# The expert gate's small tiles move into PSUM, its table behind the scatter, its diagonals to ScalarE

## The chip, the cores and the metric

The kernel runs on one core of a Trainium2 chip. The metric is the device time of one launch in microseconds (us), lower is better. The kernel before takes 684.4 us, the median of three runs (684.36 to 685.31).

## What is computed

Three stages follow each other. A clustered attention: 2 batches of 8 heads, 768 tokens, head dimension 64; a query attends only to keys whose nearest centroid (16 per head) is its own. A mixture of 8 experts with one expert per token. A second, dense layer with mish in the middle.

```python
scores = where(q_assign[..., :, None] == k_assign[..., None, :], q @ k.T / 8, -1e9)
x = softmax(scores) @ v                            # -> (1536, 512)
logits = x @ w_gate + modality_bias[modality_id]   # (1536, 8)
e_idx = argmax(logits); gate_w = softmax(logits)[e_idx]
out[e_idx == e] = gate_w * (relu(x @ w1[e]) @ w2[e])
h = out @ w_in                                     # (1536, 2048)
return (h * tanh(softplus(h))) @ w_out             # (1536, 512)
```

## The kernel before, in words

Almost every product is made of three f16 products (high part by high, low by high, high by low). In the attention, `st_step` makes 128 keys by 768 queries of scores on TensorE (L391), ScalarE takes the exponential (L393) and its f16 part (L400), GpSimd subtracts for the low part `el` (`psub`, L114), and TensorE multiplies with v (L425 to L429). After a head, `fin` divides on VectorE (L440 to L442, tile `xt`), ScalarE makes the f16 part (L445) and GpSimd the low part (L447). The centroid work of a head (`assign`) runs three heads ahead: maxima on VectorE (L286 to L292), two GpSimd operations (L295, L296), a VectorE transpose (L299), a ScalarE copy (L301) and four small DMAs into `QK` (L303).

After each pair of heads `pregate` adds a quarter of the logits of a batch: transposes, matmuls into a PSUM tile `lg`, two VectorE operations into the SBUF tile `l`. When the last quarter of a batch is in, `gate(b)` runs once for that batch of 768 tokens (128 partitions by 6 tiles). It takes the row maximum and the exponential, a one-hot `oh` of the best expert, counts with matmuls of `ones` and a triangle `tri` into the PSUM tile `rk` (L748 to L751), the gate weight `g` (L754 to L760, written into the extra columns of the token rows), and the experts' order by size (`key`, `kp`, `gt`, `st`); from these comes `pu`, the sorted row of every token (L782). Six indirect DMAs of GpSimd scatter the rows of `xb` to the DRAM tensor `dr` (L802). Besides, it makes the expert numbers `ei` (L789), by which ScalarE's or SyncE's queue loads expert weights (`w_load`, L900, L912), and the table `tab`, `nblk` and `mask` (L798 and L810 to L822), which is needed when the sorted rows are back and at the very end. The rows come back by SyncE's queue in order (L832, tile `xs`), and `sorted_mm` turns them with matmuls against two diagonal matrices `dg` of the gate weight (`diag`, L702; matmuls L713) into `xw`, the input of the experts.

`gate(0)` runs while the attention of batch 1 goes on; `gate(1)` runs after the attention, beside the experts of batch 0 (`moe1`: matmuls L1007, ScalarE L965 and L918, VectorE L969 and L922), the first matmuls of the dense layer (`h_units`, `mish` L1106 to L1115) and the conversion of `w_out` (L1027 to L1035). In the code the order of these strands is fixed by generators; within it a planner orders the instructions of each engine by its own estimate of when they are ready, except SyncE's, which stay as written. Every engine then executes its queue in that order, and an instruction that waits holds up all that is behind it.

`eps` is a PSUM pool of two banks that the attention's side work, the gate of batch 0 and the experts share; for batch 1 the gate uses a bank of the pool `ps_2`.

Of the kernel before, what the change touches and what calls it, by code (L numbers as in the profile page):

```python
# [8 lines left out]
F16 = mybir.dt.float16  # L9
F32 = mybir.dt.float32  # L10
# [3 lines left out]
AF = mybir.ActivationFunctionType  # L14
ALU = mybir.AluOpType
# [4 lines left out]
P = 128  # L20
# [4 lines left out]
def clustered_attention_moe_kernel(  # L25
# [84 lines left out]
    def eps(shape, dt=F32):  # L110
        return ps_e.tile(shape, dt, tag="e", name="eps")
# [11 lines left out]
    ident16 = cp.tile([P, P], F16, name="ident16")  # L123
# [324 lines left out]
        fin_done.add(i)  # L448
        yield

    lg_t = {}
    pre_done = set()

    def pregate(b, c):

        x = xb[b]
        last = (b, c) == (B - 1, CD - 1)

        def bank(shape, dt=F32):
            if last:  # L460
                return ps_x.tile(shape, dt, tag="x", name="x")
            return eps(shape, dt)

        xT = lp.tile([P, 2, S], F16, tag="xT", name="xT")
        for a in range(2):
            pt = bank([P, 1024], F16)
            for t in range(T):
                nc.tensor.transpose(pt[:, t * P:(t + 1) * P], x[:, t, a * DM + c * P:a * DM + (c + 1) * P], ident16)
            yield 2
            if a < XTA:  # L470
                nc.scalar.activation(out=xT[:, a], in_=pt[:, 0:S], func=AF.Copy)
            else:
                nc.vector.tensor_copy(xT[:, a], pt[:, 0:S])
            yield 1 + 3 * a
        lg = bank([P, T, 2 * E])
        for t in range(T):
            nc.tensor.matmul(lg[:, t, :], lhsT=xT[:, 0, t * P:(t + 1) * P], rhs=wg[:, c, :], start=(t == 0), stop=False, skip_group_check=True)
            nc.tensor.matmul(lg[:, t, 0:E], lhsT=xT[:, 1, t * P:(t + 1) * P], rhs=wg[:, c, 0:E], start=False, stop=(t == T - 1), skip_group_check=True)
        yield 2
        isc = 2.0 ** -14  # L480
        if c == 0:
            lg_t[b] = g1.tile([P, T, E], F32, tag="l", name="l", bufs=2)
        l = lg_t[b]
# [214 lines left out]
    def diag(xs):  # L698
        sc = xs[:, 2 * DM:].bitcast(F32)
        dg = g1.tile([P, 2, P], F16, tag="dg", name="dg", bufs=2)  # L700
        for a in range(2):
            nc.vector.tensor_scalar(out=dg[:, a], in0=ident16, scalar1=sc[:, 1 + a:2 + a], scalar2=None, op0=ALU.mult)  # L702
        return dg

    def sorted_mm(xs, dg, xr, c0, parts, pool=None):
# [16 lines left out]
    def gate(b):  # L722
# [2 lines left out]
        l = lg_t[b]  # L725
        G = lambda nm, shape, dt=F32: g1.tile(shape, dt, tag=nm, name=nm)
        V = nc.vector
        mx = G("gmx", [P, T, 1])
        V.reduce_max(out=mx[:, :, 0], in_=l, axis=AX.X)
        d = G("gd", [P, T, E])  # L730
        mb_ = mx.to_broadcast([P, T, E])
        V.tensor_tensor(out=d, in0=l, in1=mb_, op=ALU.subtract)
        nc.scalar.activation(out=d, in_=d, func=AF.Exp)
        eq = G("geq", [P, T, E])
        V.tensor_tensor(out=eq, in0=l, in1=mb_, op=ALU.is_equal)
        V.tensor_tensor(out=eq, in0=eq, in1=desc8[:, None, :].to_broadcast([P, T, E]), op=ALU.mult)
        m2 = G("gm2", [P, T, 1])
# [1 line left out]
        oh = G("goh", [P, T, E], F16)  # L739
        V.tensor_tensor(out=oh, in0=eq, in1=m2.to_broadcast([P, T, E]), op=ALU.is_equal)  # L740
        yield
        if b:
            rk = m_p["ps"].tile([P, 512], F32, tag="o", name="o", bufs=NQ)
        else:
            rk = eps([P, 512])
        r3 = rk[:, 0:T * E].rearrange("p (t e) -> p t e", e=E)
        for t in range(T):
            nc.tensor.matmul(rk[:, 64:64 + E], lhsT=ones, rhs=oh[:, t, :], start=(t == 0), stop=False, skip_group_check=True)  # L748
# [12 lines left out]
        V.memset(xf[:, :, 3], 0.0)  # L761
        yield

        cnt = rk[:, 64:64 + E]
# [7 lines left out]
        V.tensor_tensor(out=gt, in0=kp[:, None, :].to_broadcast([P, E, E]), in1=kp[:, :, None].to_broadcast([P, E, E]), op=ALU.is_gt)  # L772
# [12 lines left out]
        V.tensor_copy(c_, cnt)  # L785
# [9 lines left out]
        V.tensor_scalar(out=bst, in0=ma[:, 1:2], scalar1=-1.0, scalar2=float(S), op0=ALU.mult, op1=ALU.add)  # L795
        sel = [G(f"ge{k_}", [P, E]) for k_ in range(2)]
        for k_ in range(2):
            V.tensor_scalar(out=sel[k_], in0=key, scalar1=m8[:, k_:k_ + 1], scalar2=None, op0=ALU.is_equal)  # L798
        ab = G("gab", [P, E])
        prev = []  # L800
        for t in range(T):
# [5 lines left out]
                yield  # L807
        be = slice(b * E, (b + 1) * E)
        tl, te = tab[:, 0, be], tab[:, 1, be]
        V.scalar_tensor_tensor(out=tl, in0=sel[0], scalar=float(W), in1=st[:, 0, :], op0=ALU.mult, op1=ALU.add)  # L810
        V.tensor_tensor(out=te, in0=st[:, 0, :], in1=c_, op=ALU.add)
        V.tensor_scalar(out=ab, in0=sel[1], scalar1=-float(W), scalar2=float(S), op0=ALU.mult, op1=ALU.add)
        V.tensor_tensor(out=te, in0=te, in1=ab, op=ALU.min)
        V.tensor_tensor(out=ab, in0=te, in1=tl, op=ALU.subtract)
        V.tensor_scalar(out=ab, in0=ab, scalar1=0.0, scalar2=float(P - 1), op0=ALU.max, op1=ALU.add)
        V.tensor_copy(nblk[:, be], ab)
        V.tensor_scalar(out=nblk[:, be], in0=nblk[:, be], scalar1=7, scalar2=None, op0=ALU.logical_shift_right)
        if b:
            V.tensor_scalar(out=tab[:, :, be], in0=tab[:, :, be], scalar1=float(b * S), scalar2=None, op0=ALU.add)
        mask = G("gmask", [P, 2, OV], F16)  # L820
        V.tensor_scalar(out=mask[:, 0, :], in0=mcol, scalar1=ma[:, 0:1], scalar2=None, op0=ALU.is_lt)
        V.tensor_scalar(out=mask[:, 1, :], in0=mcol, scalar1=bst, scalar2=None, op0=ALU.is_ge)  # L822
        yield "sorted"
        ids = lp.tile([P, T], U32, tag="ids", name="ids", bufs=2)
        ids_t[b] = ids
# [187 lines left out]
    m_p = {}  # L1013
# [358 lines left out]
```

## Time and profile before

| | |
|---|---|
| median of 3 runs | 684.4 us |
| the profiled execution | 684.2 us, of which the span from first to last instruction is 682.4 us |
| TensorE (PE) busy | 622.8 us, 91% |
| VectorE (DVE) busy | 384.9 us, 56% |
| ScalarE (ACT) busy | 447.6 us, 66% |
| GpSimd (POOL) busy | 255.9 us, 37% |
| mean granted TensorE clock | 0.974 |

The times below are us from the start of the span. Busy shares are means over stages with different limits, so the stages of the two gates (about 159 to 196 us, and 324 to 363 us) are read by themselves.

### The profile page before, as it was taken

How to read it: one execution, taken by the hardware profiler on the slowest of the kernel's cores; microseconds unless marked ns; L12 is line 12 of the kernel's file. 1: busy time of each engine (PE TensorE's matmuls, PEld its weight loads, DVE VectorE, ACT ScalarE, POOL GpSimd, SP SyncE). 2: the span in 40 equal slices, each digit the busy share in tenths (PEclk: the TensorE clock that was granted, in tenths of full speed). 3: DMA queues.
4: the chain of work that ended last, by engine and by line, in shares of the span. 5: the costliest groups of instructions: out<-in, count | busy, mean ns of one | idle time of the engine just before them, and what ended most of it. 6: DMA issues, size and time to landing. Idle time of an engine off the chain costs nothing. (4 is left out here: it accounts for less than half of the span.)

```text
span 682.4 us, 13665 instructions
## 1 busy us (share of the span) xinstructions
PE 622.8 (91%) x5474; PEld 424.2 (62%) x5475; DVE 384.9 (56%) x767; ACT 447.6 (66%) x680; POOL 255.9 (37%) x226
## 2 busy tenths in 40 slices
PE   1698989989798998998989889999999999999995
PEld 1376768857476676565866556566666667676442
DVE  5768666788789799889567899622311101101000
ACT  4687798876776666665777778665655576767300
POOL 5466776875864243330421222111311232222211
PEclk9889999989789899899999999999999999999998
DMA  7632363312862243555346554212000000000000
GB/s 221 157 74 65 89 168 94 90 41 64 283 190 74 87 143 110 169 149 161 117 129 225 177 155 157 93 33 62 32 1 1 4 29 0 32 1 16 17 32 34
DMA packets 56741, 64.41 MB, mean 94 GB/s; under 512 B 10080, under 2 KB 46944, under 8 KB 56672
## 3 DMA queue, kind: packets, MB, share of 16 engines
q1 hardware_dynamic: 42064, 48.74, 24.8%
q10 hardware_dynamic: 12688, 8.42, 4.1%
q0 software_dynamic: 1920, 6.32, 2.4%
q8 instruction: 45, 0.74, 0.4%
q14 instruction: 24, 0.20, 0.1%
HBM read 46.23 MB, written 6.32 MB: 77 GB/s over the span
## 5 line engine op out<-in xcount | busy, mean ns | idle before, releaser
L114 POOL TENSOR_TENSOR el<-e,eh 128x768 f16<-128x768 f32 x64 | 106.9, 1675 | 87.2 <-ACT eh L400 48.9
L1007 PE MATMUL h<-x,win 128*128 128x256 f16 x1152 | 132.0, 273 | 0.0
L1007 PEld LDWEIGHTS <-win 128*128 128x128 f16 x1152 | 112.5, 98 | 18.6 <-issue 0.2
L1007 PEld LDWEIGHTS <-w 128*128 128x128 f16 x768 | 75.2, 99 | 68.4 <-issue 13.8
L1112 DVE SCALAR_TENSOR_TENSOR s<-s,h 128x512 f32<-128x512 f32 x48 | 30.8, 684 | 148.1 <-ACT s L1108 145.5
L1163 PE MATMUL o<-wout,xb 128*128 128x512 f16 x432 | 95.9, 379 | 0.0
L114 POOL TENSOR_TENSOR xb<-s,xb 128x1024 f16<-128x1024 f32 x18 | 40.4, 2243 | 126.7 <-ACT xb L1115 126.6
L1007 PE MATMUL eps<-xw,w 128*128 128x416 f16 x384 | 75.2, 344 | 9.5 <-DVE hT L969 5.2
L391 PE MATMUL s<-QK 128*128 128x384 f16 x320 | 79.3, 339 | 3.5 <-ACT ef L393 1.6
L351 DVE TENSOR_REDUCE mxh<-x 128x1 f32<-128x512 f32 x96 | 64.7, 681 | 17.7 <-PE x L350 17.2
L1007 PE MATMUL eps<-hT,w 128*128 128x416 f16 x384 | 73.8, 344 | 0.8 <-DVE hT L969 0.8
L1163 PEld LDWEIGHTS <-xb 128*128 128x128 f16 x432 | 42.3, 98 | 48.3
L393 ACT ACTIVATE e<-s 128x384 f32<-128x384 f32 x112 | 52.4, 489 | 23.2 <-PE s L391 19.9
L400 ACT ACTIVATE eh<-e 128x768 f16<-128x768 f32 x64 | 54.0, 846 | 1.4 <-DVE w L922 0.7
L427 PE MATMUL av<-vst,eh 128*128 128x65 f16 x384 | 46.9, 196 | 5.3 <-DVE xt L442 4.9
L425 PE MATMUL av<-vst,ef 128*128 128x65 f32 x384 | 49.6, 272 | 0.0
L425 PEld LDWEIGHTS av<-vst,ef 128*128 128x128 f32 x384 | 48.0, 192 | 1.5
L429 PE MATMUL av<-vst,el 128*128 128x65 f16 x384 | 45.1, 195 | 2.9 <-POOL el L114 2.9
L428 PE MATMUL av<-vst,eh 128*128 128x64 f16 x384 | 47.1, 197 | 0.0
L922 DVE SCALAR_TENSOR_TENSOR w<-wf,w 128x1024 f16<-128x1024 f32 x32 | 43.9, 1373 | 5.6 <-ACT w L918 5.2
L1106 ACT ACTIVATE s<-h,cst 128x512 f32<-128x512 f32 x48 | 32.9, 686 | 21.4 <-PE h L1007 21.2
L391 PEld LDWEIGHTS <-QK 128*128 128x128 f16 x384 | 34.2, 103 | 19.9 <-issue 8.5
(223 smaller groups left out, 1095.7 us busy)
## 6 DMA issues: line engine op xcount, KB each, us to landing
wf<-in_moe_w_dram ACTq DMA_DIRECT2D x16, 512.0 KB, 3.6
raw<-in_moe_w_in_dram SPq DMA_DIRECT2D x16, 512.0 KB, 3.7
raw<-in_moe_w_out_dram SPq DMA_DIRECT2D x16, 512.0 KB, 4.2
wf<-in_moe_w_dram SPq DMA_DIRECT2D x16, 512.0 KB
QK<-hl SPq DMA_DIRECT2D x32, 192.0 KB, 5.7
xs<-dr SPq DMA_DIRECT2D x12, 258.0 KB, 3.9
t<-in_k_dram SPq DMA_DIRECT2D x8, 384.0 KB, 4.4
t<-in_q_dram SPq DMA_DIRECT2D x8, 384.0 KB, 3.6
```

Of the source, the lines that this page charges most:

```text
L114: nc.gpsimd.tensor_tensor(out=out_, in0=in0, in1=in1, op=ALU.subtract)
L351: nc.vector.reduce_max(out=mx_t[i][:, t, 0:1], in_=sp, axis=AX.X)
L391: nc.tensor.matmul(sps[hf][:, 0:HS], lhsT=st[:, KA + a, kt * P:(kt + 1) * P], rhs=st[:, QA + a, hf * HS:(hf + 1) * HS], start=(a == 0), st ...
L393: nc.scalar.activation(out=e32[:, hf * HS:(hf + 1) * HS], in_=sps[hf][:, 0:HS], func=AF.Exp, scale=1.0 / float(D) ** 0.5)
L400: nc.scalar.activation(out=eh, in_=e32, func=AF.Copy)
L425: nc.tensor.matmul(av[:, t, :], lhsT=e32[:, cols], rhs=vs[:, h, :], start=(kt == 0 and t == 0), stop=(kt == T - 1), skip_group_check=True)
L427: nc.tensor.matmul(av[:, t, :], lhsT=eh[:, cols], rhs=vs[:, h, 0:NV], start=(kt == 0 and t == 0), stop=False, skip_group_check=True)
L428: nc.tensor.matmul(av[:, t, 0:D], lhsT=eh[:, cols], rhs=vs[:, h, NV:], start=False, stop=False, skip_group_check=True)
L429: nc.tensor.matmul(av[:, t, :], lhsT=el[:, cols], rhs=vs[:, h, 0:NV], start=False, stop=(kt == T - 1), skip_group_check=True)
L922: nc.vector.scalar_tensor_tensor(out=hl_[:, 1], in0=f, scalar=32.0, in1=hl_[:, 0], op0=ALU.mult, op1=ALU.subtract)
L1007: nc.tensor.matmul(out_, lhsT=wc[:, a, kk, ms], rhs=mv[:, c, kk, :], start=(i == 0), stop=(i == n - 1))
L1163: nc.tensor.matmul(pts[t], lhsT=gsl[q % 2][f // FB][:, f % FB, a, t * P:(t + 1) * P], rhs=wout[:, c, f, :], start=(f == 0 and i_ == 0), st ...
```

## The change

The gate's tiles `mx`, `eq`, `g`, `key`, `kp`, `pe`, and the counts `rk` and `cnt`, become slices of one PSUM bank; for batch 0 that is the bank of the last quarter of the logits, which `pregate` now allocates whole, for batch 1 a bank of `ps_2`. Where an operation had `key` or `kp` as both inputs, a second copy is written to SBUF, and one input is read from there (two more VectorE instructions per gate). The instructions of the table are issued after the one that makes `pu`. The two diagonals per tile of 128 rows are made by ScalarE instead of VectorE.

```diff
 def pregate(b, c):
-        lg = bank([P, T, 2 * E])
+        lgb = bank([P, 512])
+        lg = lgb[:, 0:2 * T * E].rearrange("p (t e) -> p t e", e=2 * E)
...
+        if c == CD - 1 and not b:
+            lg_b[b] = lgb
 def diag(xs):
-            nc.vector.tensor_scalar(out=dg[:, a], in0=ident16, scalar1=sc[:, 1 + a:2 + a], scalar2=None, op0=ALU.mult)
+            nc.scalar.activation(out=dg[:, a], in_=ident16, func=AF.Copy, scale=sc[:, 1 + a:2 + a])
 def gate(b):
-        mx = G("gmx", [P, T, 1])
+        bk = lg_b.get(b)
+        if bk is None:
+            bk = m_p["ps"].tile([P, 512], F32, tag="o", name="o", bufs=NQ)
+        at = [2 * T * E]
+        def R(*shape):
...                       # the next free columns of bk
+        mx = R(T, 1)
-        eq = G("geq", [P, T, E])
+        eq = R(T, E)
...
-        if b:
-            rk = m_p["ps"].tile([P, 512], F32, tag="o", name="o", bufs=NQ)
-        else:
-            rk = eps([P, 512])
+        rk, cnt = R(T * E), R(E)
...
-        g = G("gg", [P, T])
+        g = R(T)
...
-        key = G("gkey", [P, E])
-        V.scalar_tensor_tensor(out=key, in0=cnt, scalar=float(E), in1=desc8, op0=ALU.mult, op1=ALU.add)
+        key, keys = R(E), G("gkey", [P, E])
+        for k_ in (key, keys):
+            V.scalar_tensor_tensor(out=k_, in0=cnt, scalar=float(E), in1=desc8, op0=ALU.mult, op1=ALU.add)
...
-        kp = G("gkp", [P, E])
-        V.scalar_tensor_tensor(out=kp, in0=key, scalar=m8[:, 1:2], in1=key, op0=ALU.not_equal, op1=ALU.mult)
+        kp, kps = R(E), G("gkp", [P, E])
+        for k_ in (kp, kps):
+            V.scalar_tensor_tensor(out=k_, in0=key, scalar=m8[:, 1:2], in1=keys, op0=ALU.not_equal, op1=ALU.mult)
-        V.tensor_tensor(out=gt, in0=kp[:, None, :]..., in1=kp[:, :, None]..., op=ALU.is_gt)
+        V.tensor_tensor(out=gt, in0=kp[:, None, :]..., in1=kps[:, :, None]..., op=ALU.is_gt)
...
-        pe = G("gpe", [P, T, E])
+        pe = R(T, E)
...
-        V.tensor_scalar(out=pu, in0=pf, scalar1=float(b * S), scalar2=None, op0=ALU.add)
+        pi = V.tensor_scalar(out=pu, in0=pf, scalar1=float(b * S), scalar2=None, op0=ALU.add)
...
-            V.tensor_scalar(out=sel[k_], in0=key, scalar1=m8[:, k_:k_ + 1], scalar2=None, op0=ALU.is_equal)
+            with tc.issue_after(pi.ins):
+                V.tensor_scalar(out=sel[k_], in0=key, scalar1=m8[:, k_:k_ + 1], scalar2=None, op0=ALU.is_equal)
...
+        with tc.issue_after(pi.ins):
             V.scalar_tensor_tensor(out=tl, in0=sel[0], ...)
...                       # and the rest of the table, to the two masks
```

## Rows read from the trace of the kernel before

**Rows 1.** The page's first part: busy us (share of the span), number of instructions.
```profile
PE 622.8 (91%) x5474; PEld 424.2 (62%) x5475; DVE 384.9 (56%) x767; ACT 447.6 (66%) x680; POOL 255.9 (37%) x226
```
**Rows 2.** Windows: stretch, length, busy us by engine, granted clock, DMA share, GB/s.
```profile
173.00:184.00 11.00, 7.17 (x37) 3.29 (x37) 8.30 (x13) 7.06 (x11) 9.46 (x8) 0.73 0.91 276
184.00:196.00 12.00, 11.72 (x132) 8.92 (x129) 7.80 (x20) 9.00 (x17) 11.60 (x9) 0.72 0.71 250
196.00:224.00 28.00, 24.30 (x325) 19.40 (x324) 26.98 (x62) 21.34 (x42) 12.08 (x10) 0.99 0.33 85
```
**Rows 3.** PE's timeline, first gate: start, us, operation [idle before <-releaser].
```profile
171.24 0.48 PE L391 MATMUL s<-QK 128*128 128x384 f16 x2 [1.01 <-ACT e L393]
...
174.90 0.58 PE L350 MATMUL x<-QK 128*128 128x512 f16 x1 [1.55 <-DMA QK<-oT]
...
183.78 0.20 PE L429 MATMUL av<-vst,el 128*128 128x65 f16 x1 [2.28 <-POOL el L114]
```
**Rows 4.** DVE's timeline in the first gate.
```profile
160.52 1.09 DVE L732 TENSOR_TENSOR gd<-l,gmx 128x48 f32<-128x48 f32 x1
...
163.38 1.58 DVE L758 TENSOR_SCALAR gh<-gg 128x6 f16<-128x6 f32 x1
...
166.38 1.06 DVE L798 TENSOR_SCALAR ge<-gkey,gm 128x8 f32<-128x8 f32 x2
...
168.75 1.08 DVE L791 TENSOR_SCALAR gi<-gi 128x2 int32<-128x2 int32 x1
...
171.81 0.17 DVE L782 TENSOR_SCALAR gpu<-gpf 128x6 uint32<-128x6 f32 x1
```
**Rows 5.** POOL's timeline in the first gate.
```profile
163.27 1.66 POOL L114 TENSOR_TENSOR el<-e,eh 128x768 f16<-128x768 f32 x1 [1.73 <-issue]
...
171.82 0.36 POOL L295 TENSOR_SCALAR so<-seq 128x192 f16<-128x192 f32 x1 [2.01 <-DVE gpf L780]
...
172.91 1.20 POOL L802 DMA_INDIRECT dr<-xb,gpu  x1 [0.29 <-DVE nblk L816]
...
182.06 4.86 POOL L114 TENSOR_TENSOR el<-e,eh 128x768 f16<-128x768 f32 x3
```
**Rows 6.** ACT's timeline in the first gate.
```profile
165.88 0.52 ACT L445 ACTIVATE xb<-xt 128x384 f16<-128x384 f32 x1 [1.99 <-DVE xt L442]
...
169.96 0.85 ACT L301 ACTIVATE oT<-oC 128x384 f16<-128x384 f16 x1 [1.92 <-DVE gi L791]
...
184.19 1.06 ACT L918 ACTIVATE w<-wf 128x1024 f16<-128x1024 f32 x1 [2.85 <-DMA wf<-in_moe_w_dram]
```
**Rows 7.** DVE's timeline in the second gate.
```profile
329.71 0.36 DVE L798 TENSOR_SCALAR ge<-gkey,gm 128x8 f32<-128x8 f32 x2
...
331.87 0.17 DVE L782 TENSOR_SCALAR gpu<-gpf 128x6 uint32<-128x6 f32 x1
...
332.56 0.17 DVE L817 TENSOR_SCALAR nblk<-nblk 128x8 int32<-128x8 int32 x1
```
**Rows 8.** POOL's timeline in the second gate.
```profile
332.80 1.08 POOL L802 DMA_INDIRECT dr<-xb,gpu  x1 [16.65 <-DVE nblk L817]
...
345.88 2.13 POOL L114 TENSOR_TENSOR xb<-s,xb 128x1024 f16<-128x1024 f32 x1 [3.42 <-ACT xb L1115]
```
**Rows 9.** PE's timeline when the sorted rows of batch 1 are back.
```profile
345.87 0.94 PE L713 MATMUL o<-dg,xs 128*128 128x128 f16 x12 [0.89 <-DVE dg L702]
348.11 0.94 PE L713 MATMUL o<-dg,xs 128*128 128x128 f16 x12 [1.31 <-DVE dg L702]
```
**Rows 10.** DVE's timeline at the same place.
```profile
346.37 1.85 DVE L702 TENSOR_SCALAR dg<-ident,xs 128x128 f16<-128x128 f16 x2 [0.33 <-DMA xs<-dr]
```
**Rows 11.** ACT's timeline at the same place.
```profile
346.15 1.06 ACT L918 ACTIVATE w<-wf 128x1024 f16<-128x1024 f32 x1
```
**Rows 12.** Groups by line and shape: busy us, mean ns of one | idle before.
```profile
L702 DVE TENSOR_SCALAR dg<-ident,xs 128x128 f16<-128x128 f16 x24 | 6.5, 315 | 1.7 <-DMA xs<-dr 1.7
...
L717 ACT ACTIVATE xw<-o 128x128 f16<-128x128 f32 x1 | 0.3, 269 | 0.0
```

More of the change, by code (lines that the diff above doesn't have):

```diff
@@ L449, in fin @@
         yield
-    lg_t = {}
+    lg_t, lg_b = {}, {}
     pre_done = set()
@@ L727, in gate @@
         V = nc.vector
-        mx = G("gmx", [P, T, 1])
+        bk = lg_b.get(b)
[3 more added lines that the diff above has]
+        def R(*shape):
+            n_ = 1
+            for q_ in shape:
+                n_ *= q_
+            o_ = at[0]
+            at[0] += n_
+            assert at[0] <= 512
+            v_ = bk[:, o_:o_ + n_]
+            return v_ if len(shape) == 1 else v_.rearrange("p (a b) -> p a b", b=shape[1])
+        mx = R(T, 1)
         V.reduce_max(out=mx[:, :, 0], in_=l, axis=AX.X)
@@ L741, in gate @@
         yield
-        if b:
-            rk = m_p["ps"].tile([P, 512], F32, tag="o", name="o", bufs=NQ)
-        else:
-            rk = eps([P, 512])
-        r3 = rk[:, 0:T * E].rearrange("p (t e) -> p t e", e=E)
+        rk, cnt = R(T * E), R(E)
+        r3 = rk.rearrange("p (t e) -> p t e", e=E)
         for t in range(T):
-            nc.tensor.matmul(rk[:, 64:64 + E], lhsT=ones, rhs=oh[:, t, :], start=(t == 0), stop=False, skip_group_check=True)
+            nc.tensor.matmul(cnt, lhsT=ones, rhs=oh[:, t, :], start=(t == 0), stop=False, skip_group_check=True)
         nc.tensor.matmul(rk[:, 0:T * E], lhsT=tri, rhs=oh.rearrange("p t e -> p (t e)"), start=False, stop=False, skip_group_check=True)
@@ L762, in gate @@
         yield
-        cnt = rk[:, 64:64 + E]
-        key = G("gkey", [P, E])
-        V.scalar_tensor_tensor(out=key, in0=cnt, scalar=float(E), in1=desc8, op0=ALU.mult, op1=ALU.add)
+        key, keys = R(E), G("gkey", [P, E])
+        for k_ in (key, keys):
+            V.scalar_tensor_tensor(out=k_, in0=cnt, scalar=float(E), in1=desc8, op0=ALU.mult, op1=ALU.add)
         m8 = G("gm8", [P, 8])
         V.max(out=m8, in_=key)
-        kp = G("gkp", [P, E])
-        V.scalar_tensor_tensor(out=kp, in0=key, scalar=m8[:, 1:2], in1=key, op0=ALU.not_equal, op1=ALU.mult)
+        kp, kps = R(E), G("gkp", [P, E])
+        for k_ in (kp, kps):
+            V.scalar_tensor_tensor(out=k_, in0=key, scalar=m8[:, 1:2], in1=keys, op0=ALU.not_equal, op1=ALU.mult)
         gt = G("ggt", [P, E, E], F16)
-        V.tensor_tensor(out=gt, in0=kp[:, None, :].to_broadcast([P, E, E]), in1=kp[:, :, None].to_broadcast([P, E, E]), op=ALU.is_gt)
+        V.tensor_tensor(out=gt, in0=kp[:, None, :].to_broadcast([P, E, E]), in1=kps[:, :, None].to_broadcast([P, E, E]), op=ALU.is_gt)
         V.tensor_tensor(out=gt, in0=gt, in1=cnt[:, None, :].to_broadcast([P, E, E]), op=ALU.mult)
@@ L809, in gate @@
         tl, te = tab[:, 0, be], tab[:, 1, be]
[L810 to L822, printed above, removed]
+        with tc.issue_after(pi.ins):
+            V.scalar_tensor_tensor(out=tl, in0=sel[0], scalar=float(W), in1=st[:, 0, :], op0=ALU.mult, op1=ALU.add)
+            V.tensor_tensor(out=te, in0=st[:, 0, :], in1=c_, op=ALU.add)
+            V.tensor_scalar(out=ab, in0=sel[1], scalar1=-float(W), scalar2=float(S), op0=ALU.mult, op1=ALU.add)
+            V.tensor_tensor(out=te, in0=te, in1=ab, op=ALU.min)
+            V.tensor_tensor(out=ab, in0=te, in1=tl, op=ALU.subtract)
+            V.tensor_scalar(out=ab, in0=ab, scalar1=0.0, scalar2=float(P - 1), op0=ALU.max, op1=ALU.add)
+            V.tensor_copy(nblk[:, be], ab)
+            V.tensor_scalar(out=nblk[:, be], in0=nblk[:, be], scalar1=7, scalar2=None, op0=ALU.logical_shift_right)
+            if b:
+                V.tensor_scalar(out=tab[:, :, be], in0=tab[:, :, be], scalar1=float(b * S), scalar2=None, op0=ALU.add)
+            mask = G("gmask", [P, 2, OV], F16)
+            V.tensor_scalar(out=mask[:, 0, :], in0=mcol, scalar1=ma[:, 0:1], scalar2=None, op0=ALU.is_lt)
+            V.tensor_scalar(out=mask[:, 1, :], in0=mcol, scalar1=bst, scalar2=None, op0=ALU.is_ge)
         yield "sorted"
```

## The prediction, made before the changed kernel was run

> **What bounds the kernel now.** First the busy shares: TensorE is busy for 622.8 us, 91% of the span [rows 1], so any part that doesn't shorten TensorE's queue must be found in its pauses. Then the windows about the two gates: from 173 to 184 TensorE works for 7.17 of 11 us, and from there to 196 it is busy nearly throughout, but the granted clock is 0.73 and 0.72 in the two stretches [rows 2]. The clock has two levels, 1.2 and 2.4 GHz, so a mean of 0.72 says that over half of the stretch was granted the lower one, after pauses. Then TensorE's own timeline: inside the first gate it waits 1.01 us for an exponential of ScalarE, 1.55 us for a transfer of centroid rows and 2.28 us for GpSimd's low part [rows 3]. All three lie behind the gate only indirectly, through the queues of VectorE, ScalarE and GpSimd, so these were read next.
>
> VectorE shows what the change goes for. Operations on tiles of 48, 6, 16 and 2 elements per partition take 1.09, 1.58, 1.06 (two together) and 1.08 us [rows 4]; the same pair of L798 takes 0.36 in the second gate [rows 7]. Each long one ends when a GpSimd operation ends: L758 (163.38 + 1.58 = 164.96) with the low part that began at 163.27 and took 1.66 [rows 4, 5]. So a small VectorE operation whose tensors are all in SBUF waits for GpSimd's running one. I read that as a shared way into SBUF.
>
> ScalarE hands it on: L445 waits 1.99 us for `xt`, which VectorE makes behind L758; and L301 starts at 169.96 after 1.92 us of idle time that ends with L791 [rows 6]. GpSimd does so too: the scatter starts at 172.91, behind L295, which had waited 2.01 us for VectorE, and the next low parts come at 182.06, after six scatters [rows 5]; that is the 2.28 us at 183.78 [rows 3].
>
> In the second gate TensorE has work (the dense layer) until the sorted rows are back. There it waits 0.89 and 1.31 us for the diagonals [rows 9]. The second wait is the same stall: one of the two L702 that began at 346.37 ended at 348.22, after the GpSimd operation of 345.88 to 348.01 [rows 8, 10].
>
> **Part 1: small tiles in PSUM.** The stall goes where an operand is now in PSUM: `mx` (L732), `g` (L758), `key` (L798). With 0.18 us as the price of a free one (L798's pair gives 0.36) it removes 1.09 - 0.18 = 0.91, 1.58 - 0.18 = 1.40, and 1.06 - 0.36 = 0.70 us, 3.0 us of VectorE in the first gate [rows 4, 7]. L791's 0.9 stays, since `i2` remains in SBUF; so do the casts and scalings of `gh`, `ei`, `ma`, which happened to fall between GpSimd's operations and may not any more. The two added copies of `key` and `kp` cost at most 0.18 each, 0.36 per gate, and sit on the way to `pu`; at half of that, because such operations start before the one ahead has ended, 0.2. That an operation on a PSUM tile costs what it costs in SBUF is an assumption; both ends are a gain of nothing and a loss of 0.1 each over some 15 operations, 1.5 us, which I don't take, since L798's pair on SBUF has no better price to lose.
>
> In the second gate no GpSimd operation ran beside the gate's arithmetic (GpSimd had been idle for 16.65 us [rows 8]), so this part is worth nothing there and costs the 0.2.
>
> How much of the 3.0 reaches TensorE in the first gate? ScalarE's L445 can come earlier by what L732 and L758 lose, at most 2.3, but no more than its own wait of 1.99 [rows 6]. L301 stands behind it, and behind L791, which may stall as before: I bound its move by 0.3 and 1.9 and take 1.0, nearer the middle because half of the stalling operations stay. TensorE's waits of 1.01 and 1.55 hang on L393 and L301, so TensorE runs 1.0 earlier from there.
>
> **Part 2: the table behind `pu`.** Eight instructions leave the way to `pu` (two L798, six others). In the second gate that is 0.36 for the pair and at most 0.17 (L817) for each of the six [rows 7], 1.4 at the most; overlapped as above, 0.9. Less the 0.2 for the copies, `pu` is ready 0.7 earlier there. In the first gate it is 3.0 + 0.9 - 0.2 = 3.7 at the most, but the scatter is queued behind L295 and L296 [rows 5], whose input comes from VectorE's same queue; I take 2.0 between 1.0 (ScalarE's move alone) and 3.7. The six scatters then end 2.0 earlier, and so does the low part that TensorE waits for at 183.78.
>
> What is late next: TensorE, 1.0 earlier by part 1, would wait 1.3 instead of 2.28 and leave 2.0 earlier; but ScalarE stands at 184.19, where it has waited 2.85 for expert weights, and its 1.06 us hold back the exponentials behind it until 185.25 [rows 6]. That transfer is issued in ScalarE's queue behind the work of 174.90, so it moves by 1.0; and from 173 to 184 the DMA engines are busy for 0.91 of the time [rows 2], so it won't move by more. TensorE therefore keeps 1.0 and some of the rest: **1.3 us for the first gate** (bounds 0 and 3.0).
>
> In the second gate the scatter began at 332.80, 0.76 after `pu` (331.87 + 0.17) and 0.07 after L817 ended (332.56 + 0.17) [rows 7, 8]. Either the 0.76 is the way from a semaphore to GpSimd's first scatter, and it moves with `pu` by 0.7; or the scatter can't start while VectorE runs the table, and it doesn't move at all, since the table now lies wholly behind `pu`. I take 0.4.
>
> The Trainium skill speaks for the second: the page "SBUF — State Buffer", section "Who interferes with whom", says that VectorE and GpSimd share a pair of SBUF ports as a lock, that copies, casts and scalings which use both ports shut GpSimd out for the whole instruction, and that GpSimd can't write the descriptors of its own DMAs meanwhile. The 0.07 us at 332.73 agrees; the first rule, that one input in PSUM avoids the lock, is not shown by the kernel before for the gate's tiles. By that page the 0.4 would be zero, and the sum 0.4 smaller.
>
> **Part 3: diagonals by ScalarE.** Twenty-four instructions move. On VectorE the 24 take 6.5 us with one stall of 1.4 in them, so 0.22 each; a ScalarE copy of 128x128 from PSUM takes 0.269 [rows 12], 0.54 a pair. For batch 0 most pairs, I take four of six, fall in the stretch 196 to 224, where VectorE is busy for 26.98 of 28 us and ScalarE for 21.34 [rows 2]: ScalarE has 6.7 us to spare for 2.2, and VectorE gains 8 x 0.22 = 1.8. TensorE is busy 24.30 of 28 there, so at most that 1.8 comes out; ScalarE's exponentials are delayed by up to 0.54 at each pair, and four such are 2.2 lost. I take 0.2 gained.
>
> For batch 1 the stall of L702 goes, 1.85 - 0.44 = 1.4 [rows 10]. But ScalarE's queue has L918 from 346.15 to 347.21 [rows 11]; behind it the second pair is ready at 347.75, 0.36 to 0.5 before the 348.11 of [rows 9]; ahead of it, 1.3 before. The first pair loses 0.1. So 0.4 in all, and with the scatter's 0.4, **0.8 us for the second gate** (bounds: all of 0.7 + 1.3 = 2.0 gained; 0.9 lost if the first pair too is queued behind L918, as below).
>
> **Sum.** 1.3 + 0.2 + 0.8 = 2.3 us. The profiled execution took 684.2 (its span of 682.4 and 1.8 around it); 684.2 - 2.3 = 681.9. The median of the runs is 0.2 above the profiled one, so 682.1 us. It all comes through only because TensorE has no long wait for anything but its neighbours' queues later on, and these move with it.
>
> **Rivals.** *A slower kernel: ScalarE's queue takes the diagonals' wait.* A diagonal on ScalarE waits for the sorted rows, and the exponentials, expert weights and mish are behind it. If the first pair of batch 1 stands behind L918 it is ready at 347.21 + 0.54 = 347.75 instead of before 345.87: 1.9 lost, less the 1.3 of the second wait, which it absorbs, 0.6; for batch 0, 2.2 lost as above. With a first gate that yields its lower bound of 0.3 and `pu`'s 0.4 that makes 2.1 slower, 686.5, and some 685.9 if half of the pairs of batch 0 hurt. It decides where the planner puts a pair ahead of its rows' arrival, or behind a 1-us operation. For it: ScalarE is on the way to TensorE in the first gate twice [rows 3, 6]. Against: 6.7 us of spare time [rows 2].
>
> *No change that can be told.* The stalls move on to the tiles left in SBUF (L791 and its like), the weights' transfer at 184.19 holds the first gate where it is, and only 0.6 of the second gate is left: 683.8. For it: GpSimd is busy 9.46 of 11 us from 173 [rows 2] and so meets whatever VectorE issues; against: three of the four long ones are gone by construction.
>
> *The lock on the scatter,* as above, with less than the forecast in both gates (VectorE's table now beside six scatters instead of before them): 682.8.
>
> *The clock comes back.* If TensorE's pauses shrink enough that the clock stays up, the 12 us from 184 at 0.72 [rows 2] would take up to 12 x 0.28 = 3.4 less where TensorE is the limit; I take 2.6 more than the forecast: 679.5. Against: pauses of 1.0 and 1.55 us stay.
>
> **How the numbers follow.** Forecast 0.42, lock 0.10, clock 0.12, no change 0.19, slower 0.17. Faster means under 683.0 (0.2% of 684.4 is 1.4 us, about what a measurement tells from no change), slower over 685.8: nine tenths of the forecast, the clock and six tenths of the lock give 0.56 faster; 0.25 stays within; 0.19 is slower, with a little for orders of the planner that I can't see. The range that holds 8 in 10 leaves out half of the clock's case and most of the slower one: 678.8 to 685.6. The likeliest case's own range is 681.0 to 683.2.
>
> **What would show it.** Right: L732, L758 and L798 at 0.2 each beside a running GpSimd operation; L445's wait under 1; the first scatter of batch 0 near 171, of batch 1 near 332.3; TensorE's wait for the low part near 1.3; the wait of 1.31 for the second pair under 1. Wrong: VectorE operations of over 1 us on L759, L787 or L789; TensorE waiting for a diagonal from ScalarE for over 1 us; the first scatter again at the table's end. A result above 684.4 would mean that ScalarE, not VectorE, was what the gates leaned on.

## The result and the profile after

The changed kernel takes 680.25 us (median of 11 runs, 679.32 to 682.83). The kernel before, run beside it, took 687.09 (11 runs, 684.12 to 690.1; the three of the front page are among them). The ratio is **0.9911, 95% interval 0.9885 to 0.9937**: faster by 0.9%, 6.1 of 687.09 us, where 2.3 were forecast (a ratio of 0.9966). The profiled execution took 680.72.

The first part of the page, which answers to [rows 1]:

```profile
span 679.0 us, 13674 instructions
## 1 busy us (share of the span) xinstructions
PE 620.5 (91%) x5474; PEld 424.5 (63%) x5475; DVE 378.3 (56%) x747; ACT 454.6 (67%) x704; POOL 255.4 (38%) x226
```

VectorE is busy 6.6 us less, ScalarE 7.0 more: the diagonals. TensorE is busy 2.3 less with the same matmuls, which points at its clock. The stretches of [rows 2], in the same columns:

```profile
173.00:184.00 11.00, 7.47 (x58) 4.90 (x58) 8.08 (x22) 8.03 (x14) 8.35 (x7) 0.84 1.02 309
184.00:196.00 12.00, 10.44 (x144) 8.03 (x143) 10.35 (x22) 10.55 (x22) 10.63 (x9) 1.00 0.93 289
196.00:224.00 28.00, 24.20 (x315) 18.82 (x313) 23.34 (x50) 22.75 (x50) 13.54 (x10) 1.00 0.33 86
```

The clock of the first two is 0.84 and 1.00 where it was 0.73 and 0.72. Over the whole first gate, the kernel before and then the changed one:

```profile
150.00:196.00 46.00, 39.43 (x442) 28.10 (x440) 35.02 (x98) 31.54 (x57) 33.20 (x28) 0.83 0.56 175
150.00:196.00 46.00, 39.38 (x501) 30.34 (x502) 35.27 (x103) 34.06 (x64) 34.73 (x29) 0.93 0.59 175
```

TensorE is busy for as long in both, so it waits for as long too; in that time it does 501 matmuls where it did 442, at a granted clock of 0.93 where it had 0.83. This execution entered the gate 1.8 us later than that of before (`l` is ready at 161.39, before at 159.56), because TensorE was granted 1.2 GHz for 6.8 us from 54.1, where the two programs are the same. So 1.8 is to be taken off its times below. TensorE's waits that answer to [rows 3]:

```profile
172.75 0.38 PE L350 MATMUL x<-QK 128*128 128x512 f16 x1 [1.39 <-DMA QK<-oT]
...
174.96 0.48 PE L391 MATMUL s<-QK 128*128 128x384 f16 x2 [0.81 <-ACT QK L378]
...
181.08 1.44 PE L391 MATMUL s<-QK 128*128 128x384 f16 x4 [2.14 <-issue]
```

The wait of 2.28 for GpSimd's low part is gone, and the centroid rows are there 4.0 earlier (174.90 against 172.75 less 1.8). But a wait of 2.14 for the next scores has come at 181.08. The view names no releaser for it; for the same wait in e1 below (3.27 us at 181.13) it names an exponential of ScalarE. With one of 0.59 at 178.24, the waits of over 0.5 us between 165 and 190 add up to 4.9 us, where before they were 5.5 (the three of [rows 3] and one of 0.66 at 169.87). VectorE's rows of [rows 4]:

```profile
162.34 0.20 DVE L752 TENSOR_TENSOR gd<-l,eps 128x48 f32<-128x48 f32 x1
...
166.76 0.15 DVE L775 TENSOR_SCALAR gh<-eps 128x6 f16<-128x6 f32 x1
...
167.16 0.85 DVE L776 CAST xb<-gh 128x6 f32<-128x6 f16 x1
...
170.51 0.17 DVE L809 TENSOR_SCALAR gi<-gi 128x2 int32<-128x2 int32 x1
...
172.21 0.61 DVE L800 TENSOR_SCALAR gpu<-gpf 128x6 uint32<-128x6 f32 x1
...
172.74 0.35 DVE L817 TENSOR_SCALAR ge<-eps,gm 128x8 f32<-128x8 f32 x2
```

The stalls of `gd`, `gh` and `ge` are gone, as forecast; two smaller ones came on operations whose tensors are still in SBUF (L776, L800). GpSimd, for [rows 5], and ScalarE, for [rows 6]:

```profile
170.10 0.35 POOL L295 TENSOR_SCALAR so<-seq 128x192 f16<-128x192 f32 x1
...
171.16 1.64 POOL L114 TENSOR_TENSOR el<-e,eh 128x768 f16<-128x768 f32 x1 [0.27 <-ACT eh L400]
...
173.12 1.20 POOL L821 DMA_INDIRECT dr<-xb,gpu  x1 [0.33 <-DVE ge L817]
...
182.45 3.30 POOL L114 TENSOR_TENSOR el<-e,eh 128x768 f16<-128x768 f32 x2 [1.00 <-ACT eh L400]
```

```profile
165.27 0.52 ACT L445 ACTIVATE xb<-xt 128x384 f16<-128x384 f32 x1
...
168.59 0.86 ACT L301 ACTIVATE oT<-oC 128x384 f16<-128x384 f16 x1 [0.35 <-DVE oC L299]
...
171.44 1.01 ACTq L932 DMA_DIRECT2D wf<-in_moe_w_dram  x2
...
179.60 1.06 ACT L938 ACTIVATE w<-wf 128x1024 f16<-128x1024 f32 x1 [2.24 <-DMA wf<-in_moe_w_dram]
```

The last row is where ScalarE's exponentials are held while TensorE waits at 181.08: it waits 2.24 us for expert weights, and the exponentials behind it start at 180.56.

Two things here are not durations but places. A low part (171.16) now runs ahead of the first scatter; in [rows 5] none did after 168.17, and three were queued behind the sixth scatter. And L301 runs ahead of the two DMA issues of expert weights (L932); before, it ran behind them. This row of the kernel before, from the timeline of ScalarE's queue, was not among those read for the prediction:

```profile
168.87 0.96 ACTq L912 DMA_DIRECT2D wf<-in_moe_w_dram  x2
```

It ends at 169.83, and L301 began at 169.96. L301 reads only `oC`, which was ready at 168.45; so in the 1.92 us that [rows 6] puts down to L791, which happens to end at 169.83 too, ScalarE's queue loaded the expert number (`ei`, L789, at 167.75) into a register, 0.47 us from 167.9, and issued two transfers. The planner had put the instructions of all engines but SyncE into another order: of the 5,282 TensorE instructions whose order the runs below hold (weight loads left out) 1,451 stand elsewhere, of GpSimd's 220 there are 15.

In the second gate (VectorE and GpSimd for [rows 7, 8], then TensorE for [rows 9]):

```profile
326.09 0.17 DVE L800 TENSOR_SCALAR gpu<-gpf 128x6 uint32<-128x6 f32 x1
...
327.12 0.17 DVE L833 TENSOR_TENSOR tab<-tab,gab 128x8 f32<-128x8 f32 x1
...
330.70 0.17 DVE L836 CAST nblk<-gab 128x8 int32<-128x8 f32 x1
```

```profile
327.02 1.08 POOL L821 DMA_INDIRECT dr<-xb,gpu  x1 [18.50 <-DVE tab L830]
328.40 0.98 POOL L821 DMA_INDIRECT dr<-xb,gpu  x1 [0.30 <-issue]
329.69 0.98 POOL L821 DMA_INDIRECT dr<-xb,gpu  x1 [0.30 <-issue]
330.97 0.98 POOL L821 DMA_INDIRECT dr<-xb,gpu  x1 [0.30 <-issue]
```

```profile
342.19 1.89 PE L717 MATMUL o<-dg,xs 128*128 128x128 f16 x24
...
349.31 1.50 PE L717 MATMUL o<-dg,xs 128*128 128x128 f16 x24
...
355.80 0.22 PE L717 MATMUL o<-dg,xs 128*128 128x128 f16 x1 [0.78 <-ACT dg L706]
```

The first scatter starts 0.76 us after `pu` ends (326.26), exactly as before (332.04 to 332.80), and the table runs on to 331 beside the scatters (L833 lies within the first). The two waits of 0.89 and 1.31 are gone; one of 0.78 has come at a later pair.

### The profile page after: what moved, and what is told of

Same layout as the page of the kernel before. It is cut to its first block, busy times and chain, and to the rows that moved or that the text cites. A ratio compares the mean times of both kernels' runs of the same rounds, so it can differ in the third digit from the quotient of the medians.

```text
span 679.0 us, 13674 instructions
## 1 busy us (share of the span) xinstructions
PE 620.5 (91%) x5474; PEld 424.5 (63%) x5475; DVE 378.3 (56%) x747; ACT 454.6 (67%) x704; POOL 255.4 (38%) x226
## 5 line engine op out<-in xcount | busy, mean ns | idle before, releaser
L1027 PE MATMUL eps<-xw,w 128*128 128x416 f16 x384 | 72.8, 339 | 8.2 <-DVE hT L989 2.9
L1027 PE MATMUL eps<-hT,w 128*128 128x416 f16 x384 | 71.8, 339 | 1.6 <-DVE hT L989 1.6
L400 ACT ACTIVATE eh<-e 128x768 f16<-128x768 f32 x64 | 54.1, 847 | 0.8
L425 PE MATMUL av<-vst,ef 128*128 128x65 f32 x384 | 51.1, 276 | 0.0
L425 PEld LDWEIGHTS av<-vst,ef 128*128 128x128 f32 x384 | 49.8, 196 | 1.9
L350 PE MATMUL x<-QK 128*128 128x512 f16 x96 | 37.9, 404 | 8.6 <-DMA QK<-oT 5.1
L942 DVE SCALAR_TENSOR_TENSOR w<-wf,w 128x1024 f16<-128x1024 f32 x32 | 43.4, 1357 | 3.9 <-ACT w L938 3.9
```

Source lines behind the costliest of these rows:

```text
L350: nc.tensor.matmul(sp, lhsT=st[:, QA, t * P:(t + 1) * P], rhs=st[:, KA, 0:512], start=True, stop=True)
L400: nc.scalar.activation(out=eh, in_=e32, func=AF.Copy)
L425: nc.tensor.matmul(av[:, t, :], lhsT=e32[:, cols], rhs=vs[:, h, :], start=(kt == 0 and t == 0), stop=(kt == T - 1), skip_group_check=True)
L942: nc.vector.scalar_tensor_tensor(out=hl_[:, 1], in0=f, scalar=32.0, in1=hl_[:, 0], op0=ALU.mult, op1=ALU.subtract)
L1027: nc.tensor.matmul(out_, lhsT=wc[:, a, kk, ms], rhs=mv[:, c, kk, :], start=(i == 0), stop=(i == n - 1))
```

## The experiments

Three theories. *Stalls*: the prediction's, VectorE's stalls behind GpSimd were what held the first gate. *Order*: the planner's other order of the queues gains, and the place of the tiles doesn't matter in itself. *Diagonals*: their move to ScalarE carries more than was priced. Later a fourth, *bank*: batch 0's ranks no longer take one of the two `eps` banks.

To hold an order, an edge was put between each two neighbours of an engine's queue, with no wait of its own:

```python
for p, n in zip(wanted, wanted[1:]):
    tc.add_manual_dep(n, p.name, mybir.DependencyInfo(NoSync, DATA), reason="pinned order")
```

The orders are held up to the last dense matmuls, and the traces have them as they were meant to be, but for e2. No run holds a kernel unchanged in its own order, so that the edges by themselves do nothing is not shown apart; e1, which holds the changed kernel's order, is no slower than it, and e2, with edges too, is no faster than the kernel before.

All ratios are to the kernel before, run beside each, from five rounds (6 runs of e1, 9 of e11, 11 or 12 of the others); the clock is the mean granted one of 100 to 400 us in the profiled execution, from the view of busy time by stretch.

| kernel | ratio | 95% interval | clock |
|---|---|---|---|
| before | 1 | | 0.96 |
| after | 0.9911 | 0.9885 to 0.9937 | 0.99 |
| e1 after, tiles in SBUF, order held | 0.9888 | 0.9847 to 0.9930 | 0.98 |
| e2 before, two queues in after's order | 1.0075 | 1.0041 to 1.0108 | 0.95 |
| e3 after, two queues in before's order | 0.9969 | 0.9943 to 0.9995 | 0.97 |
| e4 PSUM tiles only | 0.9998 | 0.9968 to 1.0027 | 0.96 |
| e5 after, table early | 0.9925 | 0.9896 to 0.9953 | 0.98 |
| e6 after, diagonals on VectorE | 1.0034 | 1.0003 to 1.0066 | 0.96 |
| e7 diagonals only | 0.9948 | 0.9917 to 0.9979 | 0.97 |
| e8 e6, two queues in after's order | 0.9946 | 0.9913 to 0.9980 | 0.98 |
| e9 the ranks' bank only | 1.0013 | 0.9987 to 1.0039 | 0.96 |
| e10 bank and diagonals | 0.9953 | 0.9921 to 0.9984 | 0.97 |
| e11 e1, ranks in their own bank | 0.9902 | 0.9867 to 0.9937 | 0.97 |
| e12 before, whole in after's order | 0.9937 | 0.9910 to 0.9964 | 0.98 |

The gain goes with the clock. In the profiled executions TensorE is busy for 274.1 of the 300 us from 100 to 400 before, 274.1 in the changed kernel and 274.0 in e12, so it waits for 26 us in each; but it does 2,815, 2,865 and 2,847 matmuls in them, at the clocks of the table. And it isn't these executions alone: the mean granted clock of a whole run has its median at 0.973 to 0.976 over the three sets of runs of the kernel before that stand beside the experiments, at 0.984 for the changed kernel, 0.981 to 0.983 for e1, e5, e8, e11 and e12, 0.977 to 0.979 for e3, e7 and e10, and 0.973 to 0.978 for e2, e4, e6 and e9, which gain nothing. Time times clock is nearly the same throughout: in the median 669.8 us for the changed kernel, 667.8 to 670.4 before.

Where each gains: the time at which TensorE has done as much of its work (the columns that its matmuls stream, fp32 weighted by four, summed over the trace) as the kernel before at four points, less that point, in us. Each row is one execution, so what differs at 150 lies ahead of the change; where the order differs, the work done is not the same work.

| kernel | 150 | 195 | 230 | end |
|---|---|---|---|---|
| after | +2.2 | -3.7 | -3.4 | -3.6 |
| e1 | -0.6 | -3.6 | -4.6 | -5.5 |
| e2 | +2.9 | +9.8 | +10.5 | +11.0 |
| e4 | +3.3 | -2.0 | -1.2 | +4.6 |
| e6 | +0.5 | -4.0 | -3.4 | +5.7 |
| e7 | +0.6 | +0.9 | -4.3 | -3.3 |
| e12 | +0.4 | -3.7 | -3.1 | -4.2 |

**e1: the tiles back in SBUF.**

```diff
-        mx = R(T, 1)
+        mx = G("gmx", [P, T, 1])
...
-        pe = R(T, E)
+        pe = G("gpe", [P, T, E])
```

and so for `eq`, `g`, `key`, `kp`, with the order of all four engines held.

> The changed kernel with mx, eq, g, key, kp and pe back in SBUF (the extra copies kept), and every engine's instructions pinned to the order that they have in the changed kernel: only the place of the small tiles differs. The stall theory (what the change gains is VectorE's waits for GpSimd, and the TensorE pauses behind them) expects operations of about 1 us again on gd, gh and ge, and most of the gain lost: ratio to before 0.997 to 1.000. The order theory (the gain comes from the other order of instructions that the planner found for the changed program) expects the ratio of the changed kernel, 0.990 to 0.993.

Measured 0.9888, no slower than the changed kernel (the intervals overlap). Stalls are back, 3.3 us in four operations on VectorE's timeline (lines 3 higher than in the changed kernel):

```profile
160.54 1.08 DVE L755 TENSOR_TENSOR gd<-l,gmx 128x48 f32<-128x48 f32 x1
...
164.37 0.60 DVE L775 TENSOR_SCALAR gg<-gg 128x6 f32<-128x6 f32 x1
...
167.82 0.74 DVE L791 SCALAR_TENSOR_TENSOR gkpq<-gkeq,gm,gkey 128x8 f32<-128x8 f32 x1
...
170.29 0.91 DVE L799 TENSOR_TENSOR gpe<-gpe,goh 128x48 f32<-128x48 f32 x1
```

That is 2.6 more than four free ones at 0.18. So the stalls are real, PSUM removes them, and in this order of the queues removing them buys nothing that shows.

**e2 and e3: TensorE's and GpSimd's order exchanged,** the code of each kernel as it was, ScalarE and VectorE left to the planner.

```diff
+for engine in ("PE", "Pool"): hold(engine, order_of_the_other_kernel)
```

> The kernel before, with TensorE's and GpSimd's instructions pinned to the order that they have in the changed kernel. The stall theory expects no gain, 0.998 to 1.003, since every small tile is in SBUF. The order theory expects most of the gain, 0.990 to 0.995, with long VectorE operations still there.

> The changed kernel, with TensorE's and GpSimd's instructions pinned to the order that they have in the kernel before. The stall theory expects the gain to stay, 0.991 to 0.995, with VectorE's small operations short. The order theory expects 0.997 to 1.002.

The changed kernel lost two thirds of its gain in the old order (0.9969, between the two ranges that were expected), but the kernel before did not gain in the new one; it lost 0.75%, outside both ranges. The rows of e2's ScalarE (lines 3 higher), TensorE and GpSimd show why:

```profile
172.84 0.97 ACTq L915 DMA_DIRECT2D wf<-in_moe_w_dram  x2
...
173.94 0.85 ACT L304 ACTIVATE oT<-oC 128x384 f16<-128x384 f16 x1 [1.93 <-DVE gi L794]
```

```profile
186.39 0.24 PE L432 MATMUL av<-vst,el 128*128 128x65 f16 x1 [6.29 <-POOL el L117]
```

```profile
176.88 1.20 POOL L805 DMA_INDIRECT dr<-xb,gpu  x1 [0.29 <-DVE nblk L819]
...
184.68 1.65 POOL L117 TENSOR_TENSOR el<-e,eh 128x768 f16<-128x768 f32 x1
...
186.51 0.99 POOL L805 DMA_INDIRECT dr<-xb,gpu  x1 [0.17 <-issue]
```

ScalarE still issues the weights ahead of the centroid copy. And GpSimd's order was not held: the low part that in the changed kernel runs ahead of all six scatters stands behind five of them here, though the `eh` that it needs was ready at 176.42. TensorE, in an order made for an early low part, waits 6.29 us for it, over half of the 11.0 that this execution lost. So e2 is a mixture of two orders that nobody meant, and what TensorE's and GpSimd's new order would do to the kernel before by themselves is not shown by it.

**e4: the tiles in PSUM alone,** table and diagonals as before, planner free.

```diff
-        mx = G("gmx", [P, T, 1])
+        mx = R(T, 1)
...
```

> The first part of the change alone: the small tiles in PSUM and the copies of key and kp; table where it was, diagonals on VectorE, order left to the planner. The prediction's sum gives it 1.0 of the first gate's 1.3 us and a loss of 0.2 in the second: 0.999. If the tiles carry the whole measured gain it is 0.990 to 0.993.

Measured 0.9998. By the table of places it gains 5.3 us in the first gate, like the changed kernel (5.9), and loses it again, most of it after 230: the planner's order is a third one there.

**e5: the table ahead of the scatter again.**

```diff
-            with tc.issue_after(pi.ins):
+            if True:
```

> The changed kernel with its table of limits ahead of the scatter again, as before; small tiles in PSUM and diagonals on ScalarE stay. The planner's order is nearly the changed kernel's (8 of 11,133 rows differ on TensorE, 2 on ScalarE, 23 on VectorE). Order theory (the gain is the new order of the queues): ratio to before 0.988 to 0.995, like the changed kernel's 0.991. Theory of the table (it frees the scatter in both gates): the first scatters 0.7 to 2 us later than in the changed kernel, the low part and the sorted rows with them, ratio 0.995 to 0.998.

0.9925 against 0.9911, in nearly the same order. The first scatter does start 1.3 us later (174.43, where it was 173.12; the low part ahead of it runs at 171.17 and 171.16), and the ratio doesn't show it: what the late table is worth, if anything, is below what these runs tell.

**e6: the diagonals back on VectorE.**

```diff
-            nc.scalar.activation(out=dg[:, a], in_=ident16, func=AF.Copy, scale=sc[:, 1 + a:2 + a])
+            nc.vector.tensor_scalar(out=dg[:, a], in0=ident16, scalar1=sc[:, 1 + a:2 + a], scalar2=None, op0=ALU.mult)
```

> The changed kernel with the diagonals back on VectorE; tiles in PSUM and late table stay, and the planner is free. Its order is close to that of the PSUM tiles alone (which was measured at 0.9998) and far from the changed kernel's (2,436 rows differ on TensorE). Order theory: ratio 0.997 to 1.003, the gain won at the first gate and given back between 230 and 360 us. The prediction's prices: the diagonals are worth 0.6 us, so ratio 0.990 to 0.993.

Measured 1.0034: all of the gain is gone, and it goes after 230 as in e4. TensorE's longest wait between 230 and 320:

```profile
268.31 0.24 PE L427 MATMUL av<-vst,eh 128*128 128x65 f16 x1 [3.05 <-DVE xt L442]
```

and the record of the granted clock has 10.2 us at 1.2 GHz from 267.5.

**e7: the diagonals alone,** the opposite edit of e6 in the kernel before.

```diff
-            nc.vector.tensor_scalar(out=dg[:, a], in0=ident16, scalar1=sc[:, 1 + a:2 + a], scalar2=None, op0=ALU.mult)
+            nc.scalar.activation(out=dg[:, a], in_=ident16, func=AF.Copy, scale=sc[:, 1 + a:2 + a])
```

> The kernel before with the diagonals on ScalarE and nothing else, planner free. Prediction's prices: 0.6 us, ratio 0.998 to 1.000. Theory of ScalarE's diagonals (they carry the gain, by freeing VectorE where it is the fullest, and the planner's order only follows them): ratio 0.990 to 0.994. Order theory proper names no number here, since this order is a third one (1,593 rows on TensorE differ from before); where it gains, the gain should again come with fewer and shorter stretches at the lower granted clock between 160 and 230 us.

Measured 0.9948, between the two ranges that were expected, with nothing gained at the first gate and 5.2 us between 195 and 230. The kernel before waits there, TensorE's timeline:

```profile
218.44 0.83 PE L713 MATMUL eps<-dg,xs 128*128 128x128 f16 x12 [0.75 <-DVE seq L292]
...
222.75 3.78 PE L1007 MATMUL eps<-xw,w 128*128 128x416 f16 x12 [2.84 <-DVE xw L720]
```

and with the diagonals alone moved:

```profile
219.77 2.27 PE L1007 MATMUL eps<-xw,w 128*128 128x416 f16 x12
```

Both waits, 3.6 us, are gone, and the 12 matmuls behind them take 2.27 instead of 3.78, because the stretch at 1.2 GHz that the record has from 223.3 in the kernel before is gone too. VectorE, in the window of 196 to 224 as in [rows 2], is busy 24.73 us instead of 26.98:

```profile
196.00:224.00 28.00, 27.65 (x375) 22.25 (x374) 24.73 (x56) 25.73 (x58) 14.20 (x11) 1.00 0.33 86
```

This is the diagonals and a third order of the queues together; no run takes the two apart.

**e8: e6 with TensorE's and GpSimd's order held to the changed kernel's.**

```diff
 # the kernel of e6
+for engine in ("PE", "Pool"): hold(engine, order_of_after)
```

> As the kernel with the diagonals on VectorE, but TensorE's and GpSimd's order are held to the changed kernel's. If the order of TensorE's queue is what gains, and who makes the diagonals isn't: ratio 0.988 to 0.994. If the diagonals on ScalarE carry the gain: ratio 0.996 or more, with TensorE waiting for VectorE's diagonals behind other work between 196 and 360 us.

0.9946 against e6's 1.0034, with the same instructions: the order alone is worth 0.9% here. (The ratio lies between the two ranges that were expected.) Against the changed kernel's 0.9911 the intervals overlap, so what ScalarE's diagonals add in this order stays open.

**e9 and e10: the ranks' bank.** The kernel before with batch 0's ranks in the bank of the last logits, alone and with e7's diagonals; every queue keeps the order of before, or of e7.

```diff
-            rk = eps([P, 512])
+            rk = lg_b[b][:, 2 * T * E:]
```

> The kernel before with one edit: batch 0's counts and ranks (`rk`) go into the bank of the last logits in place of a bank of their own from the pool that TensorE's scores and transposes use. The instructions of every engine stay in the order of the kernel before. Bank theory (what the changed kernel gains at the first gate, some 5 to 6 us between 150 and 196, is that pool's bank, free for TensorE's scores): ratio 0.990 to 0.994. Order theory: ratio 0.997 to 1.003.

> The bank of the last kernel and the diagonals on ScalarE, nothing else; the order is that of the diagonals alone (measured at 0.9948). If bank and diagonals are two gains of their own: ratio 0.985 to 0.990, below the changed kernel's 0.991. If the order decides: ratio 0.993 to 0.997, as with the diagonals alone.

1.0013, and 0.9953 against 0.9948 without the bank. The bank is worth nothing.

**e11: e1 with the ranks in a bank of their own again.**

```diff
         rk, cnt = R(T * E), R(E)
+        if not b:
+            rkb = eps([P, 512])
+            rk, cnt = rkb[:, 0:T * E], rkb[:, 64:64 + E]
```

> The changed kernel with its small tiles in SBUF and batch 0's counts and ranks in a bank of their own again; every engine's order is held to the changed kernel's. It differs from the run with the tiles in SBUF (0.9888) by that bank alone. Bank theory: the gain at the first gate goes, ratio 0.994 to 0.999. Order theory: ratio 0.986 to 0.993.

0.9902: with the tiles in SBUF and the bank as before, the gain stays while the order stays.

**e12: the kernel before in the changed kernel's order.** No part of the change is in it; only the diagonals and the table are free to stand where the planner puts them.

```diff
 # the kernel before
+for engine in ("PE", "Activation", "DVE", "Pool"): hold(engine, order_of_after, free=("dg", "table"))
```

> The kernel before, none of its parts changed (own bank, tiles in SBUF, table ahead of the scatter, diagonals on VectorE); the order of TensorE, ScalarE, GpSimd and of all else on VectorE is held to the changed kernel's up to the last dense matmuls. Order theory: most of the gain, ratio 0.990 to 0.995 (the kernel with diagonals on VectorE in that order had 0.9946). If the bank is what gains at the first gate: ratio 0.998 to 1.004. With TensorE's and GpSimd's order alone held it was 1.0075: where that comes again, VectorE's and ScalarE's order isn't what was lacking there.

**0.9937, interval 0.9910 to 0.9964: the order by itself makes the kernel before faster.** Its rows (lines 6 higher), ScalarE, VectorE, GpSimd and TensorE:

```profile
167.25 0.84 ACT L307 ACTIVATE oT<-oC 128x384 f16<-128x384 f16 x1
...
170.68 1.02 ACTq L918 DMA_DIRECT2D wf<-in_moe_w_dram  x2
```

```profile
161.11 1.08 DVE L738 TENSOR_TENSOR gd<-l,gmx 128x48 f32<-128x48 f32 x1
...
170.12 1.61 DVE L799 CAST gma<-gi 128x2 f32<-128x2 int32 x1
```

```profile
170.06 1.64 POOL L120 TENSOR_TENSOR el<-e,eh 128x768 f16<-128x768 f32 x1
...
173.74 1.21 POOL L808 DMA_INDIRECT dr<-xb,gpu  x1 [2.04 <-DVE gpu L788]
```

```profile
171.46 0.38 PE L356 MATMUL x<-QK 128*128 128x512 f16 x1 [1.24 <-DMA QK<-oT]
```

VectorE stalls as long as ever (1.08, 1.61), and the first scatter starts 0.8 us *later* than before's 172.91, in an execution that enters the gate 0.6 later. Yet the centroid copy runs at 167.25 instead of 169.96, ahead of the weights' issue; the rows that TensorE needs are there at 171.46 instead of 174.90; and a low part goes ahead of the scatters. TensorE's waits are not shorter for it: one of 2.42 us comes at 180.89, as in the changed kernel at 181.08. What the record of the clock shows is 6.8 us at 1.2 GHz between 160 and 400 us instead of 20.4.

## Why the prediction was half right

**Direction and range held, the size and its main cause did not.** 680.25 lies between 678.8 and 685.6, but by ratio the gain is 6.1 us, and the interval (0.9885 to 0.9937) shuts out the forecast's 0.9966. That the range held is in part luck: its lower end is a ratio of 0.9918 to the 684.4 that it was worked out from, and 0.9911 is below that. The kernel before took 687.09 beside the changed one, and the two errors met.

*Part 1, the first step that failed.* "A small VectorE operation whose tensors are all in SBUF waits for GpSimd's running one" holds for the operations that were read: 1.09 became 0.20, 1.58 became 0.15, and e1 brings stalls back. It is too wide as a rule: in e1 a TENSOR_REDUCE from SBUF to SBUF (L774) took 0.19 us at 164.14 and a MAX8 (L788) 0.16 at 167.09, each beside a GpSimd operation of 1.65. The Trainium skill, page "SBUF — State Buffer", section "Who interferes with whom", says that a VectorE instruction with at most one SBUF input, outside the modes that use both ports, does not contend with GpSimd. `gd` agrees: with two inputs in SBUF it took 1.09, with one 0.20. But the next step, that 1.0 of the 3.0 us reaches TensorE through L445 and L301, is refuted by e1, which keeps the gain with 2.6 us of stalls. (e4, without them, ends where the kernel before does, but in an order of its own.) L445's wait did go (under 1 was expected), and L301 did come earlier, by 3.2 and not 1.0, but because it changed places with the weights' issue: in e12 it does so with the stalls in place. Here the trace was misread: [rows 6] names L791 for an idle time that a register load and two DMA issues in ScalarE's own queue filled, which the prediction didn't look up.

*Part 2.* The scatter came where forecast (173.12, or 171.3 less the late start, "near 171"), and the low part's wait is gone, where 1.3 was to be left. That was no chain: in e12 the scatter is later and the gain is there. The low part now stands ahead of the scatters. What the prediction had as late next did hold TensorE: ScalarE waits 2.24 us for expert weights, and TensorE 2.14 at 181.08. In the second gate `pu` to scatter is 0.76 in both kernels, so the scatter moved with `pu`, as one of the two readings had it; e5 prices the late table at nothing that can be told. One price was misread: of the six instructions that were put at 0.17 at most, the two masks (L821, L822) take 0.25 in the second gate. And two bounds don't agree with themselves: the first gate's lower one is 0 in the sum and 0.3 in the slower rival, the second gate's loss 0.9 in the sum and 0.6 where it is worked out. The misread price is worth 0.16 at the most, and neither bound enters the forecast.

*Part 3, the mis-sized term.* 0.2 us for batch 0 rested on "ScalarE has 6.7 us to spare, VectorE gains 1.8, at most that comes out". e7 measures 3.6 us of TensorE's waits and a stretch of low clock, 0.5% of the time, with the order that came with it. The wait of 2.84 for VectorE's `xw` at 222.75 stood in the trace, in the stretch whose window showed VectorE at 26.98 of 28 us, and was not looked up. How much of it is the diagonals' is open: in e12, with the diagonals on VectorE, the same wait is 1.17 us (221.36), and in the changed kernel 1.17 too (220.99). For batch 1 the signs came as written: the first pair without a wait, one wait of 0.78 after it.

*The rivals.* ScalarE's queue as the loser didn't happen: no wait of over 0.8 us for a diagonal. The lock on the scatter didn't show with the table: in the second gate six scatters took 0.98 to 1.08 with its operations beside them. In the first gate scatters that began beside VectorE's work on the expert weights were longer, 2.01 us at 176.19 before (L922 from 176.13) and 1.67 at 178.50 after (L942 from 178.10). That is no rule either, since one of e12 that began beside the same work took 0.98 (180.52). The clock came back, as that rival had it, and by time times clock it is the whole gain, but for another reason than the one given: between 160 and 400 us the record has 3.4 us at 1.2 GHz (from 180.4) instead of 20.4 (from 172.1, 185.8, 223.3 and 284.8), and TensorE's pauses did not shrink. In e12 nothing but the order was set, and the clock rose with it (0.981 against 0.974, medians of the runs), so the order brings the clock. Which of its pauses do it isn't shown. The planner's order was named in half a sentence ("orders of the planner that I can't see") and was the largest term.

What stays open: which single move of the new order does it (the centroid copy ahead of the weights' issue and the low part ahead of the scatters are the two that the rows show; e3 comes nearest to parting them, with the copy ahead at 166.69, the low part behind six scatters at 178.44 and TensorE's order of before, and has a third of the gain); why the planner chose it; and how much of the diagonals' gain is left on top of the order (e12's 0.9937 against e1's 0.9888 and e11's 0.9902, with intervals that touch). e1 had the best ratio, but no version is shown to beat the changed kernel.

## What to carry to other kernels

Where a planner orders the queues, an edit changes the order of things that it never touches. Before a gain is put down to the edit, compare the order of every queue, run the old code in the new order, all queues of it, and read from the trace whether the order was held: e2's was not, in one place, and that place cost 6.29 us. Where the waits add up to as much as before, look at the granted clock, over all runs and not one. And before pricing an idle time, look at what the engine's own queue did in it, DMA issues and register loads too: here the releaser that the view named had only ended at the same moment.

## What was not expected of the hardware

The granted clock fell in executions of the same instructions at different places: the changed kernel's profiled run had 6.8 us at 1.2 GHz from 54.1 us, that of before none there. The kernel before, in the 32 runs beside e9 to e12, spread from 682.26 to 690.41 us, the changed one, in 11, from 679.32 to 682.83. Small operations on PSUM slices cost what they cost in SBUF (`gd` 0.20, the pair of L817 0.35 against 0.36 for L798), and a 128x128 scaling by ScalarE takes 0.40 us by itself and 0.68 a pair, where the prediction had 0.54 a pair from a 128x128 copy out of PSUM.
